# Loading a 512-element vector as four rows and transposing it with one matmul, in place of 512 loads of four bytes

## The chip, the cores and the metric

The kernel runs on one core of a Trainium2 chip. The metric is the device time of one execution in microseconds (us). Most repeated executions of one kernel scatter by a few tenths of a microsecond; some kernels here scatter by 2 to 4 us. "Faster" or "slower" needs 2%, which is 5.6 us here.

Engines are named as in the profile: PE is TensorE (matmuls; PEld is its weight loads), DVE is VectorE, ACT is ScalarE, POOL is GpSimd, SP is SyncE, which issues most DMA transfers. A "q" after the name (SPq, ACTq) means the engine's queue of instructions, where DMA issues stand.

## The reference, cut to what matters

```python
def _attn_ref(q, k, v):                    # 8 batches, 8 heads, 576 tokens, 64 wide
    q_s = softmax(q, axis=-1)              # written out in the reference
    k_s = softmax(k, axis=2)
    kv = np.einsum('bhsd,bhse->bhde', k_s, v)
    return np.einsum('bhsd,bhde->bhse', q_s, kv)

def _moe_ref(x, g_ln, w_ch1, w_ch2):       # x: 8 x 576 x 512
    mu, var = mean and variance of x over its last axis
    xn = (x - mu) / np.sqrt(var + 1e-06) * g_ln     # g_ln: 512 numbers
    ch = np.maximum(xn @ w_ch1, 0.0) @ w_ch2        # 512 -> 2048 -> 512
    return x + ch
```

## The kernel before

The kernel folds `g_ln` into the first weight matrix: row c of `w_ch1` is multiplied by 16 times g[c], and the mean over the rows is subtracted from the result, so that the tokens themselves need no centring. For that, g must lie down the partitions of SBUF, 128 numbers in each of four columns. The kernel fetches it that way, with four DMA transfers of 128 elements of four bytes:

```python
plan.add("POOL", 1.5, lambda: make_identity(nc, ident), w=["ident"])       # never read
...
for ko in range(KO1):                                                      # KO1 = 4, P = 128
    plan.add("ACT", 0.4, lambda ko=ko: nc.scalar.dma_start(
        g_sb[:, ko : ko + 1], moe_g_ln[ko * P : (ko + 1) * P, None]), w=[("g", ko)])
plan.add("POOL", 4.5, lambda: nc.gpsimd.tensor_scalar_mul(g_sb, in0=g_sb, scalar1=GS),
         r=[("g", ko) for ko in range(KO1)], w=[("g", ko) for ko in range(KO1)])
```

The kernel contains a planner. Every piece of work is added as a task with an engine, a believed duration, the keys it reads and writes, and a class `cls`. When all tasks are known, a greedy list scheduler walks through believed time and fixes the order of every engine; only then are the instructions emitted.

`fill` then puts matmuls of zeros ("fillers") into TensorE's believed idle times at the start; they are meant to keep its clock up.

Tasks:

```python
nc.tensor.matmul(pa[..], ek[..], vb[..])              # L379  key-value product ("kv"), into two banks pa
nc.vector.reciprocal(rz[..], pa[..])                  # L386  1/sum of exp(k)
nc.vector.tensor_scalar_mul(kve[..], pa[..], rz[..])  # L393  scaled kv
nc.vector.reduce_sum(zq[:, hf], eh, axis=AX.X)        # L331  row sums of exp(q), 1.35 us
nc.vector.tensor_tensor(w1, w1, nm, op=ALU.subtract)  # L292  subtracts the mean from a block of w1
nc.sync.dma_start_transpose(eqT[u], eq[u])            #       transposes exp(q) of batch 1, by DMA
nc.tensor.matmul(pa[..], kve[..], eqT[..])            # L405, L428 (last rows): transposed x of batch 1
nc.vector.tensor_copy(xsT[..], pa[..])                # L416  evacuates it
w2_sums: T[0..3] = differences of blocks of w2        # L566  three on VectorE, one on GpSimd
nc.tensor.matmul(pg[gis[j]], hT[..], w2_sb[..])       # L677  second layer of batch 0, 16 groups of 4 matmuls
nc.tensor.matmul(bank[gi], w1_sb[..], xt[..])         # L535  first layer
```

The kernel uses eight banks of PSUM, the memory that matmuls write: `pa[0..3]` and `pg[0..3]`. From batch 1 on, the second layer is done in another form (`mm2_split`, L615), in which VectorE evacuates (L625).

The softmax here doesn't subtract the row's maximum and nothing guards it: scores larger than these inputs give would overflow.

Of the kernel before, what the change touches and what calls it, by code (L numbers as in the profile page):

```python
# [12 lines left out]
FP32 = mybir.dt.float32  # L13
FP16 = mybir.dt.float16
# [125 lines left out]
def kernel(  # L140
# [10 lines left out]
    nc = tc.nc  # L151
# [3 lines left out]
    P = 128  # L155
# [5 lines left out]
    KO1 = DM // P  # L161
# [3 lines left out]
    GS = 16.0  # L165
# [4 lines left out]
    def sb(shape, dt, name):  # L170
        return persist.tile(shape, dt, name=name, tag=name)
# [1 line left out]
    w1_sb = sb([P, KO1, DH], FP16, "w1_sb")  # L173
    w2_sb = sb([P, KO2, DM], FP16, "w2_sb")
    g_sb = sb([P, KO1], FP32, "g_sb")
    ident = sb([P, P], FP16, "ident")
    zero = sb([P, 512], FP16, "zero")
    ones = sb([P, P], FP16, "ones")
    eps = sb([P, 1], FP32, "eps")
# [27 lines left out]
    pa = [psum.tile([P, 512], FP32, name=f"pa{i}", tag=f"pa{i}") for i in range(4)]  # L207

    plan = Plan()
# [9 lines left out]
    def init():  # L219
        plan.add("ACT", 1.3, lambda: nc.scalar.add_instruction(mybir.InstLoadActFuncSet(  # L220
            name=nc.get_next_instruction_name(), engine=mybir.EngineType.Activation, act_func_set_id=6)), cls=-1)
        plan.add("DVE", 0.3, lambda: nc.vector.memset(zero.bitcast(U32), 0), w=["zero"])  # L222
        plan.add("DVE", 0.1, lambda: nc.vector.memset(eps, 1e-6 * GS * GS), w=["eps"])
        plan.add("DVE", 0.1, lambda: nc.vector.memset(ones, 1.0 / DM), w=["ones"])
        plan.add("POOL", 1.5, lambda: make_identity(nc, ident), w=["ident"])
        for i in range(2):
            plan.add("POOL", 0.2, lambda i=i: nc.gpsimd.memset(vb[i][:, :, :, :, D], 1.0), w=[("vb", i, h, e) for h in range(2) for e in range(2)])
        for ko in range(KO1):
            plan.add("ACT", 0.4, lambda ko=ko: nc.scalar.dma_start(
                g_sb[:, ko : ko + 1], moe_g_ln[ko * P : (ko + 1) * P, None]), w=[("g", ko)])  # L230
        plan.add("POOL", 4.5, lambda: nc.gpsimd.tensor_scalar_mul(g_sb, in0=g_sb, scalar1=GS),
                 r=[("g", ko) for ko in range(KO1)], w=[("g", ko) for ko in range(KO1)])


    gate = [(), None]
# [465 lines left out]


    init()
    warmed = warm(12)
    state = {"eqT": (), "ev": []}
# [83 lines left out]
```

## Time and profile before

| | before |
|---|---|
| median of 3 runs (the fourth came with the result) | 281.96 us (281.94 to 282.53) |
| span of the profiled execution | 280.7 us |
| TensorE busy | 269.3 us (96%) |
| VectorE busy | 205.1 us (73%) |
| GpSimd busy | 12.6 us (5%) |

From the page of the kernel before, the 40 slices of the span (7.0 us each): busy tenths of TensorE and VectorE, and the rate of the DMA engines.

```profile
PE   8988898999999997999999999999999999999994
DVE  0988999899869874986598659966986683641573
GB/s 190 386 388 386 390 388 202 313 297 258 385 186 149 251 354 63 149 145 381 141 149 104 388 177 149 156 392 122 149 86 21 131 149 2 0 36 116 1 2 151
```

TensorE is full almost everywhere. From the second to the sixth slice the DMA engines bring weights and inputs at 386 to 390 GB/s, and VectorE is nearly full too; TensorE is busy as well, in part with fillers.

The timeline of the kernel before in its first microseconds (start, duration, engine, line, operation, tiles; in brackets the engine's idle time before the instruction and what ended it):

```profile
0.74 2.02 ACTq L229 DMA_DIRECT2D g_sb<-in_moe_g_ln_dram  x4
...
2.23 0.47 SPq L238 DMA_DIRECT2D stg<-in_q_dram  x1
5.77 0.89 SPq L238 DMA_DIRECT2D stg<-in_moe_w_ch_dram  x2
5.77 1.16 ACT L329 ACTIVATE eq<-stg 128x1152 bf16<-128x1152 f32 x1 [3.78 <-DMA stg<-in_q_dram]
...
9.34 1.39 POOL L231 TENSOR_SCALAR g_sb<-g_sb 128x4 f32<-128x4 f32 x1 [7.19 <-DMA g_sb<-in_moe_g_ln_dram]
```

The first q lands at about 5.75 us (ScalarE's exp starts at 5.77). GpSimd waits 7.19 us for g and is done at 10.73. The first block of w1 that needs g lands at 11.85 us, so GpSimd's multiply is on nobody's critical path.

VectorE's timeline a little later, in the kernel before:

```profile
11.41 0.16 DVE L386 RECIPROCAL rz<-pa 128x1 f32<-128x1 f32 x1
11.61 0.28 DVE L393 TENSOR_SCALAR kve<-pa,rz 128x64 f16<-128x64 f32 x1
...
12.34 0.16 DVE L386 RECIPROCAL rz<-pa 128x1 f32<-128x1 f32 x1
12.42 1.33 DVE L331 TENSOR_REDUCE zq<-eq 128x18 f32<-128x1152 bf16 x1
...
16.91 1.22 DVE L292 TENSOR_TENSOR w_sb<-w_sb,cp 128x2048 f16<-128x2048 f16 x1
```

The first mean is subtracted from w1 by 18.13 us.

TensorE's timeline in the stage, the second layer of batch 0, in the kernel before:

```profile
37.31 5.34 PE L677 MATMUL pg<-w_sb,hT 128*128 128x512 f16 x24
42.58 0.90 PE L379 MATMUL pa<-vb,ek 64*64 64x65 f16 x72
43.42 4.49 PE L677 MATMUL pg<-w_sb,hT 128*128 128x512 f16 x20
49.14 0.63 PE L405 MATMUL pa<-eqT,kve 64*64 64x512 bf16 x8 [1.23 <-DMA eqT<-eq]
...
51.37 0.25 PE L428 MATMUL pa<-eqT,kve 64*64 64x64 bf16 x6 [0.49 <-DVE xsT L416]
51.55 3.63 PE L677 MATMUL pg<-w_sb,hT 128*128 128x512 f16 x16
55.01 3.19 PE L535 MATMUL pa<-xsT,w_sb 128*128 128x512 f16 x14
```

The stage starts at 37.31 us. After 44 matmuls, which are 11 of the 16 groups, TensorE waits 1.23 us for the DMA transpose of exp(q), then 0.49 us for VectorE's evacuation (L416), and does the last 16 matmuls after that. At 55.01 us it can begin block 1, the first layer of batch 1.

### The profile page before, as it was taken

The page shows a single profiled execution, that of the slowest core. Times are in us where ns is not written, and L with a number is a line of the kernel's source. Part 1 is how long each engine was busy: PE and PEld are TensorE (multiplying, and loading weights), DVE is VectorE, ACT ScalarE, POOL GpSimd, SP SyncE. Part 2 cuts the span into 40 slices and gives each one's busy share as a digit, 9 for nine tenths or more (in the row PEclk, how much of TensorE's full clock was granted, in tenths as well). Part 3 has the DMA queues.
Part 4 walks back from the last instruction along what each step waited for, and adds up shares of the span by engine and source line. Part 5 has one row for each costly group of instructions (what it writes and reads, how often), then busy time and mean ns, then how long its engine had stood idle before and what let it go on. Part 6 is the DMA issues. An engine that isn't in the chain of part 4 may idle for free.

```text
span 280.7 us, 5656 instructions
## 1 busy us (share of the span) xinstructions
PE 269.3 (96%) x2317; PEld 163.8 (58%) x2317; DVE 205.1 (73%) x408; ACT 163.9 (58%) x267; POOL 12.6 (5%) x17
## 2 busy tenths in 40 slices
PE   8988898999999997999999999999999999999994
PEld 3443344445864486546854785478447844874583
DVE  0988999899869874986598659966986683641573
ACT  3567793298887594569655865695565067006500
POOL 2115007000000000000000000000000000000000
PEclk9999999999999999999999999999999999999998
DMA  6999999999958992569655995797543650013004
GB/s 190 386 388 386 390 388 202 313 297 258 385 186 149 251 354 63 149 145 381 141 149 104 388 177 149 156 392 122 149 86 21 131 149 2 0 36 116 1 2 151
DMA packets 58522, 55.36 MB, mean 197 GB/s; under 512 B 37248, under 2 KB 37760, under 8 KB 58496
## 3 DMA queue, kind: packets, MB, share of 16 engines
q1 hardware_dynamic: 57776, 54.86, 68.6%
q8 instruction: 18, 0.29, 0.4%
q10 hardware_dynamic: 720, 0.13, 0.3%
q14 instruction: 8, 0.07, 0.1%
HBM read 36.70 MB, written 9.44 MB: 164 GB/s over the span
## 4 chain that ended last, share of the span: by engine, by line
PE 73%; DMA 13%; DVE 9%; ACT 1%; POOL 1%; issue 1%; DVEq 0%
PE pg L535 37%; PE pg L615 28%; DMA stg<-in_moe_w_ch_dram 6%; DMA x<-xsT 5%; PE pg L677 3%; DVE T L566 2%; DMA stg<-in_q_dram 2%; DVE S L551 2%; DVE bst L487 1%; PE pa L379 1%; PE pa L615 1%; PE pa L535 1%; POOL w_sb L271 1%; DVE ot L625 1%; PE pa L405 1%
## 5 line engine op out<-in xcount | busy, mean ns | idle before, releaser
L498 ACT ACTIVATE hT<-pg 128x512 f16<-128x512 f32 x134 | 79.4, 596 | 73.4 <-PE pg L535 72.6
L535 PE MATMUL pg<-xsT,w_sb 128*128 128x512 f16 x488 | 108.1, 379 | 0.5 <-DVE w_sb L292 0.5
L535 PEld LDWEIGHTS <-w_sb 128*128 128x128 f16 x568 | 54.8, 98 | 65.6 <-DVE w_sb L292 1.5
L615 PEld LDWEIGHTS <-S 128*128 128x128 f16 x512 | 49.7, 98 | 5.9
L615 PEld LDWEIGHTS <-hT 128*128 128x128 f16 x384 | 37.0, 98 | 10.5 <-issue 5.0
L615 PE MATMUL pg<-T,S 128*128 128x256 f16 x368 | 42.5, 273 | 0.1
L551 DVE TENSOR_TENSOR S<-hT 128x1024 f16<-128x1024 f16 x32 | 22.0, 688 | 25.9 <-ACT hT L498 25.8
L625 DVE SCALAR_TENSOR_TENSOR cp<-pg,st,x 128x256 f32<-128x256 f32 x46 | 20.2, 479 | 13.7 <-PE pg L615 12.9
L615 PE MATMUL pg<-w_sb,hT 128*128 128x256 f16 x248 | 29.3, 273 | 0.0
L625 DVE SCALAR_TENSOR_TENSOR ot<-pg,st,cp 128x256 f32<-128x256 f32 x47 | 20.5, 478 | 9.9 <-PE pg L615 9.7
L487 DVE BATCH_NORM_STATS2 bst<-x 128x6 f32<-128x512 f16 x36 | 24.0, 668 | 4.9 <-DMA x<-xsT 4.8
L331 DVE TENSOR_REDUCE zq<-eq 128x18 f32<-128x1152 bf16 x16 | 21.5, 1344 | 5.7 <-ACT eq L329 5.7
L329 ACT ACTIVATE eq<-stg 128x1152 bf16<-128x1152 f32 x16 | 18.7, 1172 | 6.2 <-DMA stg<-in_q_dram 6.2
L335 DVE TENSOR_TENSOR eq<-eq,rzq 128x1152 bf16<-128x1152 bf16 x16 | 21.7, 1357 | 0.5
L356 ACT ACTIVATE ek<-stg 128x1152 bf16<-128x1152 f32 x16 | 18.6, 1169 | 1.5 <-DMA stg<-in_k_dram 1.5
L418 ACT CAST xsT<-pa 128x512 f16<-128x512 f32 x28 | 14.5, 595 | 4.7 <-PE pa L405 4.7
L368 ACT CAST vb<-stg 128x1152 f16<-128x1152 f32 x14 | 16.3, 1171 | 0.6 <-DMA stg<-in_v_dram 0.6
L615 PE MATMUL pg<-T,hT 128*128 128x256 f16 x120 | 14.4, 273 | 2.2 <-DVE ot L625 2.2
L615 PE MATMUL pg<-w_sb,S 128*128 128x256 f16 x128 | 15.3, 273 | 0.0
L696 PE MATMUL pg<-zero 128*128 128x512 f16 x47 | 13.4, 441 | 1.2 <-DVE zero L222 1.2
L677 PE MATMUL pg<-w_sb,hT 128*128 128x512 f16 x64 | 14.5, 380 | 0.0
L535 PE MATMUL pg<-xT,w_sb 128*128 128x512 f16 x64 | 14.0, 379 | 0.0
(67 smaller groups left out, 176.2 us busy)
## 6 DMA issues: line engine op xcount, KB each, us to landing
stg<-in_q_dram SPq DMA_DIRECT2D x16, 576.0 KB, 5.4
stg<-in_k_dram SPq DMA_DIRECT2D x16, 576.0 KB, 7.4
stg<-in_v_dram SPq DMA_DIRECT2D x16, 576.0 KB, 8.2
out_dram<-ot SPq DMA_DIRECT2D x33, 256.0 KB, 3.6
stg<-in_moe_w_ch_dram SPq DMA_DIRECT2D x16, 512.0 KB, 10.2
out_dram<-ot SPq DMA_DIRECT2D x1, 512.0 KB, 2.8
x<-xsT SPq DMA_TRANSPOSE x8, 6.7
out_dram<-ot SPq DMA_DIRECT2D x1, 128.0 KB, 2.7
```

Source lines behind the costliest of these rows:

```text
L329: plan.add("ACT", act_t(QW), lambda: nc.scalar.activation(e.rearrange("p j (s d) -> p s j d", s=2), sv(s), AF.Exp), r=sk(s), w=[("eq", u, ...
L331: plan.add("DVE", dve_t(QW), lambda: nc.vector.reduce_sum(zq[:, hf], eh, axis=AX.X), r=[("eq", u, hf)], w=[("zq", hf)], cls=qcls, after=sums_)
L335: plan.add("DVE", dve_t(QW), lambda: nc.vector.tensor_tensor(eh, eh, rzq[:, hf].to_broadcast([P, 2 * JT, D]), op=ALU.mult), r=[("rzq", hf) ...
L356: plan.add("ACT", act_t(QW), lambda: nc.scalar.activation(ek[u][:, hf].rearrange("p j (s d) -> p s j d", s=2), sv(s), AF.Exp), r=sk(s), w= ...
L368: plan.add("ACT", act_t(QW), lambda: nc.scalar.copy(vd, va), r=sk(s), w=[("vb", u, hf, i) for i in range(2)], cls=cls, slack=late, after=exps)
L487: plan.add("DVE", dve_t(512), lambda j=j: nc.vector.bn_stats(bst[:, j, :], x[:, j, :]), r=[(xk, j)], w=[("bst", j)], cls=cls, slack=2.0 if ...
L498: nc.scalar.activation(hT[:, m, :], bank, AF.Relu)
L535: nc.tensor.matmul(bank[gi], w1_sb[:, ko, m * P : m * P + P], xt[:, ko], start=(ko == 0), stop=(ko == KO1 - 1))
L551: plan.add("DVE", dve_t(256 * n, 2), lambda: nc.vector.tensor_tensor(S[i][:, ks], a, b, op=op), r=r, w=sk(i), cls=0.3 if k0 else 0.45)
L615: nc.tensor.matmul(g[i][0], fa(k, i), fb(k), start=(first and k == 0 and (i == 0 or g[0][1] != g[1][1])), stop=(last and k == HK - 1), ski ...
L625: nc.vector.scalar_tensor_tensor(dst[:, i, :], in0=g[i][0], scalar=sti[:, 4, 2 * t0 + i : 2 * t0 + i + 1], in1=src[:, i, :], op0=ALU.mult, ...
L677: nc.tensor.matmul(pg[gis[j]], hT[:, kk, j * P : j * P + P], w2_sb[:, kk, :], start=(kk == 0), stop=(kk == KO2 - 1))
```

## The change

The intent is to have g loaded as four rows of 512 contiguous bytes, to turn them with one small matmul, to let VectorE multiply by 16 straight from PSUM, and to drop an identity that nobody reads.

```diff
-    ident = sb([P, P], FP16, "ident")
+    g_row = sb([KO1, P], FP32, "g_row")
+    ident_g = sb([KO1, KO1], FP32, "ident_g")
...
-        plan.add("POOL", 1.5, lambda: make_identity(nc, ident), w=["ident"])
+        plan.add("POOL", 0.8, lambda: make_identity(nc, ident_g), w=["ident_g"])
...
-        for ko in range(KO1):
-            plan.add("ACT", 0.4, lambda ko=ko: nc.scalar.dma_start(
-                g_sb[:, ko : ko + 1], moe_g_ln[ko * P : (ko + 1) * P, None]), w=[("g", ko)])
-        plan.add("POOL", 4.5, lambda: nc.gpsimd.tensor_scalar_mul(g_sb, in0=g_sb, scalar1=GS),
-                 r=[("g", ko) for ko in range(KO1)], w=[("g", ko) for ko in range(KO1)])
+        plan.add("ACT", 0.4, lambda: nc.scalar.dma_start(g_row, moe_g_ln.rearrange("(ko ki) -> ko ki", ki=P)), w=["g_row"], land=2.5)
+        plan.add("PE", 0.1, lambda: nc.tensor.transpose(pa[3][:, :KO1], g_row, ident_g), r=["g_row", "ident_g"], w=[("pa", 3)])
+        plan.add("DVE", 0.2, lambda: nc.vector.tensor_scalar_mul(g_sb, in0=pa[3][:, :KO1], scalar1=GS),
+                 r=[("pa", 3)], w=[("g", ko) for ko in range(KO1)])
```

## The prediction

> **What bounds the kernel before.** (1) From 5 to 42 us the loads: the 40 slices show 386 to 390 GB/s, and loads of w1 and w2 land one every 1.36 us (11.85, 13.22, ... 45.53 us). (2) VectorE is nearly full from 7 to 52 us. (3) From 30.4 us TensorE works almost without a gap; the timeline shows idle times of 1.23 us (at 49.14, waiting for the DMA transpose of eq), 0.49 (51.37), 0.41 (81.38) and 1.84 (111.65, an evacuation that stands on VectorE behind statistics waiting for a DMA transpose). A gain at the start counts only where it moves the ends of those gaps.
>
> **Removed.** Four issues on ScalarE's queue (0.49 us each), 512 packets of 4 bytes (9 ns each), a GpSimd multiply (1.39 us, ending at 10.73) and an unused identity. GpSimd's wait for g (7.2 us) cost nothing: g_sb is ready at 10.73 us, and the first w1 lands at 11.85.
>
> **Added.** One load of 4 rows, one tiny matmul, one VectorE multiply of 128x4 (0.2 us). In the order of instructions they stand behind 26 filler matmuls and the cast of vb, so g_sb is ready at about 10.7 us again: no gain from g itself.
>
> **DMA start.** Between 2.5 and 4.75 us the trace has packets of q and of g one for one (18/18, 19/19, 12/12, 14/14 per quarter microsecond), which fits the Trainium skill, "DMA: Bandwidth & Descriptors", section on queues, rings and completion order: an engine takes turns between queue rows packet by packet. The loads need 3 us from their first packet to full rate; after later pauses 1.25 to 1.75. If g's packets do that, all loads come about 0.8 us earlier (estimate); if it is only a cold start, 0. I take 0.5.
>
> **Moved.** The kernel's planner believed GpSimd busy for 4.5 us; without that it reorders everything up to 115 us. Propagating the trace's durations through the new order:
> - First block of w1: subtracting its mean now stands on VectorE behind the scaling of block 1 (landing at 20.1), so first-layer matmuls start later (about 2 us at 32 us).
> - That is absorbed, for TensorE waits at 49.1 us anyway for the transpose of eq, which the DMA queue ends 3.56 us after the last w2 load (45.53).
> - But only 9 instead of 11 of the 16 groups of the first second-layer product (0.87 us each) now stand before that wait. The 1.23 us gap grows to 2 us or more and 1.74 us of work comes after it; the 0.49 us gap goes. Token block 1 starts at 56.1 instead of 55.0 us, less the DMA gain.
> - At 81 us a product fills the 0.41 us gap; an earlier transpose of x takes 0.2 us off the 1.84.
>
> Sum: +1.1 (to 1.6) - 0.5 - 0.4 - 0.2, about +0.2.
>
> **Prediction:** 282.2 us, 80% within 280.8 to 283.6. Chances: faster 0.03, same 0.94, slower 0.03.
>
> **What would show it.** First q load landing at about 5 us instead of 5.75, all landings earlier by the same; g_sb written near 10.7; the first subtraction of the mean ending near 21 instead of 18.1; TensorE's gap at 49 us over 2 us; none at 81; the gap at 112 slightly smaller; steady stages unchanged (28 us per block).
>
> **What would make it wrong.** A DMA start unmoved (+0.5) or moved by over 1 us; the transpose of eq issued after 44.5 us, so that the delay isn't absorbed (+1 to 2); x transposes that close the 1.84 us gap (-1.5).

## More of the kernel before

```python
# Plan.order(), cut
t0 = max(free[eng], min(ready[i] for i in lst))                  # engine's next start
c = min((i for i in lst if ready[i] <= t0 + 1e-9), key=...)      # best class among the READY tasks
```

So a task of the best class that is ready 0.1 us too late loses its turn to whatever is ready.

SyncE issues four loads by 2.70 us and its fifth only at 5.77.

## The result, and the profile after

| | before | after |
|---|---|---|
| median, runs of the same rounds | 282.12 us (281.94 to 282.53, 4 runs) | 283.50 us (283.32 to 284.15, 4 runs) |
| ratio of fast runs, 95% interval | | 1.0051 (1.0031 to 1.0071): "same" |
| span of the profiled execution | 280.7 us | 281.5 us |

Ratios are the mean time of one kernel's fast runs over the mean of the other's fast runs of the same rounds, so they are not quite the ratio of the medians. The range of the prediction held, by 0.1 us. But the change was to be about neutral, and it costs 1.4 us. The interval excludes 1, so there is something to explain.

The first microseconds after:

```profile
0.74 0.55 ACTq L229 DMA_DIRECT2D g_row<-in_moe_g_ln_dram  x1
...
2.85 1.14 SPq L238 DMA_DIRECT2D stg<-in_moe_w_ch_dram  x2
...
4.67 1.16 ACT L329 ACTIVATE eq<-stg 128x1152 bf16<-128x1152 f32 x1 [2.68 <-DMA stg<-in_q_dram]
...
9.34 0.22 PE L230 MATMUL pa<-ident_g,g_row 4*128 4x4 f32 x1
...
9.60 0.16 DVE L231 TENSOR_SCALAR g_sb<-pa 128x4 f32<-128x4 f32 x1
```

The load does what it should: q lands 1.1 us earlier, SyncE issues on without a stop (the fifth load at 2.85 instead of 5.77 us; these two turn out to have different causes, see before_1dma), and g is ready at 9.76 us instead of 10.73.

VectorE after:

```profile
11.19 1.34 DVE L331 TENSOR_REDUCE zq<-eq 128x18 f32<-128x1152 bf16 x1
...
13.26 0.16 DVE L386 RECIPROCAL rz<-pa 128x1 f32<-128x1 f32 x1
13.46 0.28 DVE L393 TENSOR_SCALAR kve<-pa,rz 128x64 f16<-128x64 f32 x1
...
20.15 1.22 DVE L292 TENSOR_TENSOR w_sb<-w_sb,cp 128x2048 f16<-128x2048 f16 x1
```

Here the row sums stand before the reciprocals. They start 1.2 us earlier than before, but the reciprocal is 1.85 us later, and the mean of w1's first block is subtracted by 21.37 us instead of 18.13. This is another order of work, not a slower instruction.

TensorE in the second layer of batch 0, after:

```profile
38.37 2.75 PE L677 MATMUL pg<-w_sb,hT 128*128 128x512 f16 x12
...
43.71 3.63 PE L677 MATMUL pg<-w_sb,hT 128*128 128x512 f16 x16
49.00 0.63 PE L405 MATMUL pa<-eqT,kve 64*64 64x512 bf16 x8 [1.67 <-DMA eqT<-eq]
...
51.03 0.25 PE L428 MATMUL pa<-eqT,kve 64*64 64x64 bf16 x6 [0.28 <-DVE xsT L416]
51.21 5.35 PE L677 MATMUL pg<-w_sb,hT 128*128 128x512 f16 x24
56.40 1.89 PE L535 MATMUL pa<-xsT,w_sb 128*128 128x512 f16 x8
```

The stage starts 1.06 us later, the transposed exp(q) arrives at the same time as before (49.00 against 49.14), only 36 matmuls instead of 44 stand before that wait, and 24 instead of 16 after L428. Block 1 starts at 56.40 us, 1.39 us later. The sum is exact: eight matmuls more after L428 are 5.19 - 3.46 = 1.73 us from the start of that row of matmuls to block 1, and L428 was released 0.34 us earlier.

The rest of the kernel gives a part back. The wait of 0.41 us at 81 us is gone, that at 112 us is 1.56 instead of 1.84 us, and from the start of block 3 to the last matmul both kernels take the same (163.72 and 163.73 us). The starts of the stages in the traces that are compared below:

| trace | stage starts | L405 | L428 released | block 1 | block 3 | last matmul ends |
|---|---|---|---|---|---|---|
| before | 37.31 | 49.14 | 51.37 | 55.01 | 113.39 | 277.12 |
| before_again | 37.23 | 49.49 | 51.29 | 54.94 | 112.82 | 276.65 |
| after | 38.37 | 49.00 | 51.03 | 56.40 | 113.84 | 277.56 |
| bank | 36.57 | 48.43 | 50.64 | 54.28 | 112.03 | 275.84 |
| late_kv | 38.91 | 49.48 | 51.57 | 56.94 | 114.20 | 277.93 |
| before_late2 | 38.43 | 49.05 | 51.69 | 55.33 | 113.49 | 277.21 |

### The profile page after: what moved, and what is told of

The parts are those of the page before. It is cut to its first block, busy times and chain, and to the rows that moved or that the text cites. A ratio compares the mean times of both kernels' runs of the same rounds, so it can differ in the third digit from the quotient of the medians.

```text
span 281.5 us, 5669 instructions
## 1 busy us (share of the span) xinstructions
PE 270.8 (96%) x2327; PEld 164.7 (58%) x2327; DVE 204.9 (73%) x409; ACT 163.9 (58%) x267; POOL 11.0 (4%) x16
## 4 chain that ended last, share of the span: by engine, by line
PE 83%; DMA 12%; DVE 3%; ACT 1%; issue 0%; SPq 0%; DVEq 0%
PE pg L535 41%; PE pg L615 31%; DMA stg<-in_moe_w_ch_dram 4%; PE pg L677 3%; DMA x<-xsT 3%; DMA eqT<-eq 2%; PE pa L379 2%; DMA stg<-in_k_dram 2%; PE pa L405 2%; PE pa L615 1%; PE pa L535 1%; DVE w_sb L292 1%; PE pg L513 1%; DVE w_sb L274 1%; DVE cp L284 0%; PE pa L428 0%
## 5 line engine op out<-in xcount | busy, mean ns | idle before, releaser
L696 PE MATMUL pg<-zero 128*128 128x512 f16 x56 | 15.6, 433 | 1.2 <-DVE zero L223 1.2
L677 PE MATMUL pg<-w_sb,hT 128*128 128x512 f16 x64 | 14.7, 380 | 0.0
```

The source lines that it names most:

```text
L677: nc.tensor.matmul(pg[gis[j]], hT[:, kk, j * P : j * P + P], w2_sb[:, kk, :], start=(kk == 0), stop=(kk == KO2 - 1))
```

## The experiments

### First the planner: why is there another order at all?

The prediction said that the order changed because the planner no longer believes GpSimd busy for 4.5 us. This can be tried without a chip, by building. With that belief changed to anything from 0.2 to 3.5 us, the kernel before keeps its order on all engines. The step is wrong.

The cause is the PSUM bank. The change borrows `pa[3]` for the transpose of g, and the first kv product needs `pa[2]` and `pa[3]`. In the planner's own times kv then starts at 10.53 instead of 10.33 us and its reciprocal is ready at 11.17 instead of 10.97. The row sums are ready at 11.08. Before, the reciprocal was ready first and went first; now it is 0.09 us late, the scheduler gives VectorE to the row sums for 1.35 us, and much of what follows falls into another place. The traces of before and late_kv differ in their order up to about 85 us, not up to 115 as the prediction had it. Two builds show it. They also separate the two effects of the change, so both were run.

**bank** is the new load with the transpose in `pg[0]`, which nobody needs then. Its order on every engine is that of before, except for g's own instructions and one filler.

```diff
-  nc.tensor.transpose(pa[3][:, :KO1], g_row, ident_g)  ... w=[("pa", 3)]
+  nc.tensor.transpose(pg[0][:, :KO1], g_row, ident_g)  ... w=[("pg", 0)]
```

**late_kv** is the old load with the first kv product believed ready 0.2 us later. Its order is that of after.

```diff
-  slack=SLACK if steady else 0.2
+  slack=SLACK if steady else 0.4 if kind == "first" and hs == [0] else 0.2
```

They ran together with each kernel unchanged.

> The new load of g with the transpose put into bank pg[0] instead of pa[3]; by the built programs every engine then has the order of the kernel before (g's own instructions and fillers aside). Theory (the loss comes from the new order, which hangs on the borrowed bank, and the new load itself is a small gain): 281.5 to 282.1 us, that is 0.0 to 0.6 us below before and about 1.5 us below the changed kernel; first q load lands at 4.65 us as in the changed kernel; matmuls of the first layer run on without a break from about 30.0 us. Rival 1 (the new load, the float32 matmul or its place among the fillers costs by itself): 283 us or more, as the changed kernel. Rival 2 (all is noise between builds): within 0.3 us of both, no sign.

> The kernel before, loads of four bytes and all, with one number of its planner changed (it believes the first kv matmul 0.2 us later), which by the built programs gives every engine the order of the changed kernel. Theory (order alone loses): 283.3 to 284.2 us, 1.3 to 2.0 us above before, slightly above the changed kernel; first q load at 5.75 us; break of TensorE at 49 us 1.3 us or more, unbroken first-layer matmuls from about 31.8 us. Rival 1 (the load costs): 282.1 us as before. Rival 2 (noise): within 0.3 us of before.

> The kernel before, unchanged, for a second trace and for what two builds of one program differ by: ratio 1.000 within 0.002. Theory and rivals agree, except that rival 2 (noise) would have it differ by 1 us or more.

> The changed kernel, unchanged, in five rounds beside the others: 283.5 us, 1.2 to 1.6 us above before. First q load again at 4.65 us; the loads' lead over before again shrinks from 1.1 us at the first to about 0.4 us by 12 us (if the shrinking was chance, it stays near 1 us).

| kernel | load, order | median (range) | ratio to before, 95% |
|---|---|---|---|
| before (11 runs) | old, old | 282.10 (281.68 to 282.45) | |
| bank | new, old | 281.79 (281.53 to 281.99) | 0.9989 (0.9977 to 1.0001) |
| late_kv | old, new | 283.32 (282.95 to 283.50) | 1.0041 (1.0028 to 1.0054) |
| before_again | old, old | 281.96 (281.89 to 282.47) | 0.9999 (0.9987 to 1.0011) |
| after_again | new, new | 284.49 (282.70 to 285.90) | 1.0085 (1.0050 to 1.0119) |

The order alone costs 1.2 us in the medians (late_kv against before) and the load alone gains 0.3 us. bank differs from the changed kernel in nothing but the bank, and late_kv from before in nothing but the order. So the loss is an accident of scheduling, which the change triggered by borrowing a bank; the new load is innocent. Its own gain of 0.3 us is not clear of noise in the totals, for the interval of bank reaches 1.0001.

TensorE in late_kv, which has the old load, in the second layer of batch 0:

```profile
38.91 2.75 PE L677 MATMUL pg<-w_sb,hT 128*128 128x512 f16 x12
...
49.48 0.63 PE L405 MATMUL pa<-eqT,kve 64*64 64x512 bf16 x8 [1.59 <-DMA eqT<-eq]
...
51.57 0.25 PE L428 MATMUL pa<-eqT,kve 64*64 64x64 bf16 x6 [0.35 <-DVE xsT L416]
51.75 5.35 PE L677 MATMUL pg<-w_sb,hT 128*128 128x512 f16 x24
```

Again 24 matmuls stand after L428, as in after.

after_again spread over 3.2 us, which was not expected. Three of its six runs had a mean granted clock of 0.993 or 0.994, and these took 285.34 to 285.90 us; the others, at 0.997 to 1.0, took 282.70 to 283.65. (A mean of 0.997 need not matter: the trace of before has it too, and its half-rate stretch starts at 279.12 us, after the last matmul.) The trace of after_again is one of the three. Two stretches of it around 21 us (busy time of TensorE and its count of matmuls, then the granted clock, the DMA share and the rate):

```profile
18.00:21.30 3.30, 1.55 (x41) 1.00 1.05 388
21.30:24.71 3.41, 3.29 (x8) 0.50 1.05 387
```

For 3.41 us TensorE ran at half clock, after it had been idle from 18.31 to 19.63 us and again before 21.42. The Trainium skill, "TensorE: Matmul & The Clock Gate", section "What's actually happening", describes this: a free-running window of about 3.4 us, and half rate after an idle one. The window's length and the half rate agree with the trace. That the stretch before must be idle does not: TensorE was busy for 1.55 of its 3.30 us. Some runs are hit and some are not, as the six show, and other kernels are hit too (one run of before at a clock of 0.994 took 283.20 us). The four runs of the first measurement of after had clocks of 0.999 to 1.0, so its 283.50 us contain hardly any of this, and the 1.4 us must be explained without it.

### Is it the number of groups before the wait?

The prediction put the loss down to 9 instead of 11 groups before the wait at 49 us. In the planner, the believed landing time of that transpose decides how many groups are put ahead. Believed 2.6 instead of 0.6 us, after has 11 groups there, and bank has 14.

```diff
-  land=3.5 if steady else 0.6
+  land=3.5 if steady else 2.6        # transpose of exp(q), batch 1
```

> The changed kernel with one number of its planner changed (it believes that the first transpose of eq lands 2 us later), so that again 11, not 9, of the 16 groups of the first second-layer product stand before TensorE's wait for that transpose; the order up to there stays the changed kernel's. Theory (the loss is what the order puts behind that wait): the break at 49 us falls from 1.67 us to under 0.4, the first matmul of token block 1 starts at about 55 us instead of 56.4, time 281.9 to 282.6 us where no clock drop falls in, that is near the kernel before. Rival (the later start of the first layer, 31.45 against 30.39 us, is the loss): the time stays at 283.3 us or more.

> The kernel of run bank with the same planner number changed, which puts 14 of the 16 groups before the wait. Theory: the break of 1.26 us at 48.4 us goes, at most 0.5 us comes back because fewer matmuls cover the evacuations after it; 280.3 to 281.2 us, 0.6 to 1.5 below bank. Rival (a later wait sets the pace, as the statistics at 111 us): 281.5 us or more, with the break there larger by what was gained.

Both missed. after_l26 took 285.40 us (284.55 to 288.71), 1.0139 (1.0102 to 1.0176) of before; bank_l26 took 281.55 us (280.90 to 281.77), 0.9980 (0.9967 to 0.9993). In both the wait for the DMA is gone. But in after_l26 a longer wait for VectorE stands right behind it. TensorE in after_l26:

```profile
49.05 0.63 PE L405 MATMUL pa<-eqT,kve 64*64 64x512 bf16 x8
...
52.83 0.25 PE L428 MATMUL pa<-eqT,kve 64*64 64x64 bf16 x6 [2.03 <-DVE xsT L416]
53.01 5.31 PE L677 MATMUL pg<-w_sb,hT 128*128 128x512 f16 x16
```

and VectorE in after_l26, just before the evacuation that L428 waits for:

```profile
50.42 0.88 DVE L566 TENSOR_TENSOR T<-w_sb,T 128x512 f16<-128x512 f16 x2
51.22 0.42 DVE L566 TENSOR_TENSOR T<-w_sb 128x512 f16<-128x512 f16 x1
51.74 0.43 DVE L566 TENSOR_TENSOR T<-w_sb,T 128x512 f16<-128x512 f16 x1
52.09 1.28 DVE L416 CAST xsT<-pa 128x512 f16<-128x512 f32 x2
```

L405 was done with its eight matmuls by 49.7 us. The evacuation stood behind differences of w2 which nobody needs before the next stage: the planner, believing the transpose late, had put them ahead. The 16 matmuls after it take 5.31 us instead of 3.63 (before), because in this trace the clock is at half from 53.30 to 56.71 us, again after a stretch that was not idle (1.38 us busy in the 3.41 us before). At full rate block 1 would start at about 56.5 us (an estimate: 53.01 plus the 3.46 us of before), as in after. So this run moved the loss and did not remove it; its two runs at a clock of 1.0 still took 284.55 and 284.83 us, and what costs them the rest is open. In bank_l26 the same number moved the waits to 57.8 us (1.19 us, VectorE's output work) and 75.4 us (0.89 us). A belief changed by hand doesn't only move the one task it belongs to. Block 1 of bank_l26 did start at 53.03 instead of 54.28 us, as expected; the gain was returned within 22 us, in waits for VectorE.

**after_fill** put eight fillers into the idle times of after at 18 to 21 us.

```diff
+  if kind == "first" and hs == [1]: zeros(pg[3], True)(6)    # ahead of the second kv product
+  if m == 0: zeros(pg[3], True)(2)                           # ahead of the first layer's first matmuls
```

> The changed kernel with eight more filler matmuls, six ahead of the second kv product and two ahead of the first-layer matmuls, where TensorE stood idle for 1.05 to 1.31 and 0.55 us. Theory of the spread (the runs at 285 to 286 us are those in which the granted clock falls to a half for one window of 3.4 us after that idle stretch): no run with a mean clock under 0.996, all runs within 283.0 to 283.9 us. Rival (the spread comes from the DMA or elsewhere): again some runs above 285 us.

It missed too: it took 283.80 us (283.51 to 285.40). The idle times at 19.6 and 21.4 us are gone from its trace, but one of six runs still had a clock of 0.994 and took 285.40, and two at 0.999 and 1.0 took 284.64 and 284.09, so the clock is not all of the spread. One run of six at a low clock against three of six is too little to call the half-rate windows rarer, and they are not the explanation of the 1.4 us.

### Is it the number of transfers or the number of elements that holds the start up?

**before_1dma** fetches the same 512 elements of four bytes with one transfer.

```diff
-  for ko in range(KO1): nc.scalar.dma_start(g_sb[:, ko : ko + 1], moe_g_ln[ko * P : (ko + 1) * P, None])
+  nc.scalar.dma_start(g_sb, moe_g_ln.rearrange("(ko ki) -> ki ko", ki=P))
```

> The kernel before with the 512 elements of four bytes loaded by one DMA instead of four; every engine keeps its order. Theory (the packets of four bytes slow the start of the loads): q lands again at about 5.7 us, time 282.0 us as before. Rival (the four issues, or the waits of the queues that four more DMAs in flight bring, slow it): q lands at 4.4 to 4.7 us, as with the four rows. A q between them would say that both do.

It took 282.11 us (281.95 to 282.57), 1.0008 (0.9995 to 1.0020). The first q lands at 5.61 us, as in the old load (5.49 to 5.77 in four traces) and not as in the new (4.42 to 4.99 in seven). Yet SyncE's fifth load is issued at 2.79 us, as in the new load: the stop of SyncE goes with the four transfers, the late q with the small elements. The rates say the same. In before the DMA engines move 138 GB/s from 2.50 to 4.25 us, in after 366; in before_1dma, where the small elements come a little later, the rate falls to 56 from 4.00 to 4.50 us. So the many small elements delay the first loads, not the issuing. This agrees with what the prediction quoted from the Trainium skill, "DMA: Bandwidth & Descriptors", section on queues, rings and completion order: engines take turns between queues packet by packet. In before the trace shows such turns (18 packets on each of the two queues from 2.75 to 3.00 us); in before_1dma, from 4.00 to 4.25 us, they are 9 to 76, so the turns need not be one for one.

### Does the wait absorb a late start of the stage?

After these runs a rival theory looked strong. In four traces of the old order, block 1 started 17.70 or 17.71 us after the start of the stage; in four of the new, 18.03 us. If this distance was rigid, because VectorE's work in this stage hangs on the stage's own kv product, then the later start would pass through in full, and the prediction's word "absorbed" would be the failed step. **before_late** tests this: five matmuls of zeros, 1.1 us, ahead of the stage, in the kernel before.

```diff
   for kk in range(k0, k0 + 4):        # preceded, for c == 0, k0 == 0, j == 0, by
+      zeros(pg[gis[0]], True)(5)
```

> The kernel before with five zero matmuls (about 1.1 us of TensorE) put directly ahead of the first group of the first second-layer product, and nothing else; this imitates the later start of that product in the changed kernel without the other load and without the other order. Theory A (the chain of VectorE work that begins with the key-value product inside this stage sets when block 1 may start, and it moves with the start of the stage): the stage starts at about 38.4 instead of 37.3 us, the distance from there to block 1 stays 17.70 us, and the kernel takes about 1.1 us longer at block 3 as well as at the end of the chain of TensorE, about 283.0 to 283.3 us in all. Theory B, that of the prediction (the wait at 49 us is for a DMA that lands at its own time, so it absorbs a late start): the wait shrinks from 1.2 to 1.7 us to under 0.6 us, the distance is about 16.6 us, and the time is within 0.2 us of before.

The four timed runs took 282.37 us in the median (282.15 to 282.68), 1.0011 (0.9999 to 1.0024). The profiled execution took 1583 us, with every 128x512 matmul at about 1.7 us throughout, instead of one every 0.216 us. The clock is listed as 1.0, but this trace holds no record of a granted clock at all (its page has no PEclk line). It shows no stage and is left out; what happened in it is open. So the kernel ran once more.

> The same kernel as before_late, once more, for a trace: the profiled execution of before_late ran every matmul some eight times too slow, so that it shows no stage, while its four timed runs took only about 0.3 us more than before, where 1.1 us of work was added. What is to be told apart is where the other 0.8 us went. Theory A1: the late start passes the wait at 49 us in full (17.70 us from the start of the stage to block 1, which starts at about 56.0 us) and is taken up later, in the waits at 81 and 111 us (block 3 then starts at 113.1 us or earlier, as against 112.8 to 113.4 us in the two traces of before). Theory B: the wait at 49 us takes it up (distance about 16.6 us, block 1 starts at about 55.0 us). Time again 282.2 to 282.6 us under both.

It took 282.39 us (282.32 to 282.61), 1.0007 (0.9993 to 1.0021). TensorE in before_late2 (what is L677 in the other kernels is L679 here, two inserted lines later):

```profile
38.43 5.34 PE L679 MATMUL pg<-w_sb,hT 128*128 128x512 f16 x24
...
49.05 0.63 PE L405 MATMUL pa<-eqT,kve 64*64 64x512 bf16 x8
...
51.69 0.25 PE L428 MATMUL pa<-eqT,kve 64*64 64x64 bf16 x6 [0.90 <-DVE xsT L416]
51.87 3.63 PE L679 MATMUL pg<-w_sb,hT 128*128 128x512 f16 x16
55.33 2.97 PE L535 MATMUL pa<-xsT,w_sb 128*128 128x512 f16 x13
```

The stage starts at 38.43 us, as late as in after. The wait of 1.23 us before L405 has shrunk to 0.09 us, VectorE takes up the rest by being late itself, and block 1 starts at 55.33 us, only 0.32 us later than before: 16.90 us after the stage's start. The rival theory falls, and the prediction's "absorbed" holds for 0.8 of 1.1 us. The constant distance had misled: it was constant because nothing in those traces moved one end alone.

This run also gives the cleanest comparison. before_late2 and after start the stage together (38.43 and 38.37) and get the transposed exp(q) together (49.05 and 49.00). after is released at L428 0.66 us earlier, and yet starts block 1 1.07 us later. The two groups that the new order left for later, 1.73 us, make the whole difference.

### VectorE and GpSimd in the same stage

VectorE's differences of w2 (L566) take 0.42 us, but some take 1.37. The group of this line in bank (number of instructions; shortest, median and longest in ns; first and last start):

```profile
L566 DVE TENSOR_TENSOR T<-w_sb,T x8: 411/446/1369, 43.4 to 51.1; 128x512 f16<-128x512 f16 x8
L566 POOL TENSOR_TENSOR T<-w_sb x4: 1156/1297/1337, 42.4 to 47.0; 128x512 f16<-128x512 f16 x4
```

**bank_t3** and **bank_t3_l26** let VectorE compute GpSimd's four differences too, in bank and in bank_l26.

```diff
-  eng, e = ("POOL", nc.gpsimd) if i == 2 else ("DVE", nc.vector)
+  eng, e = "DVE", nc.vector
```

> bank with the four differences of w2 that GpSimd computes given to VectorE. Theory A (two engines compete for SBUF there: three differences on VectorE take 1.37 us instead of 0.42 us while GpSimd runs its own): every difference on VectorE takes 0.41 to 0.45 us, VectorE's chain between the key-value product and the evacuations of the transposed x gets about 1.6 us shorter (2.85 less, 1.26 more), the 0.47 us wait before the ninth rows' product at 50.6 us goes, and block 1 starts about 0.45 us earlier, 17.25 us after the start of the stage. In the total 0.3 to 0.5 us, 281.3 to 281.5 us. Rival: the long ones are long for another reason (their operands), stay at 1.37 us, and block 1 starts over 1 us later because VectorE has more to do.

> bank_l26 (14 groups of the first second-layer product ahead of the wait) with the four differences of w2 that GpSimd computes given to VectorE. In bank_l26 the gain was given back, 1.19 us at 57.8 us and 0.89 us at 75.4 us, where TensorE waited for VectorE. If VectorE is late there because of the competition with GpSimd, the first of these falls below 0.4 us and the kernel takes 280.2 to 281.0 us, about 0.5 to 1.0 us less than bank_l26. If not, it stays at 281.5 us.

The same group in bank_t3:

```profile
L566 DVE TENSOR_TENSOR T<-w_sb x8: 415/417/419, 33.3 to 54.8; 128x512 f16<-128x512 f16 x8
L566 DVE TENSOR_TENSOR T<-w_sb,T x8: 393/416/419, 43.6 to 55.2; 128x512 f16<-128x512 f16 x8
```

With GpSimd quiet, none is long. That part is shown, and it agrees with the Trainium skill, "SBUF — State Buffer", section "Who interferes with whom": a VectorE instruction with two inputs in SBUF contends with a GpSimd instruction that reads SBUF. The wait before L428 disappeared and block 1 started 17.27 us after the stage's start (17.25 had been expected). The total did not follow: 282.38 us (281.32 to 283.54), 1.0012 (0.9988 to 1.0036). Two of its six runs had a clock of 0.993 or 0.994 and took 283.54 and 283.30; the other four took 281.32 to 282.74, about as bank does. A new wait of 2.49 us for VectorE stands at 76.5 us in its trace. The build shows that the planner had moved other work too; that this makes the wait is argued, not shown. bank_t3_l26 had a median of 281.53 us over all six runs; one run at a clock of 0.95 is put aside as slow, and the five fast ones took 280.40 to 281.75 us, 0.9969 (0.9953 to 0.9985). Its profile is that slow run, so its waits are not compared and its expectation, which was about a wait, stays undecided. It is as good as bank_l26 within the intervals. These two are the only kernels whose interval lies below 1 against before, by 0.2 and 0.3%.

### The end of the kernel

One term was found by reading the traces only. From the start of the last store's issue, which is on ScalarE's queue, to the end of the span, the traces with four transfers of g on that queue take 3.05 to 3.07 us (four traces), and those with one transfer 3.25 to 3.54 us (eight traces in the fast state; after and bank 3.4). The data of that store go out equally fast, the last packet 1.8 us after the issue starts, in before, late_kv, before_1dma, after, bank and bank_l26; what follows is the program's own closing instructions on all engines. before_1dma has the old elements and one transfer, and takes 3.4 us: so it goes with the number of transfers, not with the size of the elements. Why the closing takes longer is open.

## Why the prediction was right or wrong

Its range held; its centre of 282.2 us was 1.3 us low. That 283.50 lies under the upper end of 283.6 is in part luck: the second measurement of the same kernel, after_again, came to 284.49 us. The parts, one by one:

- **"What would show it", first item: q at about 5 us.** Right in direction; it came earlier still, at 4.65 instead of 5.75 us. "All landings earlier by the same" was wrong. The first w1 lands at 11.47 instead of 11.85 us, the last w2 at 45.05 instead of 45.53. A lead of 1.1 us becomes one of 0.4 to 0.5. The traces show where it goes: from 9 to 10 us the loads run at 226 to 251 GB/s in all seven fast traces of the new load, and at 386 to 407 in the five fast traces with the old elements. Why the rate falls there is open. The prediction had named a move of q by over 1 us as something that would make it wrong; q did move by 1.10, and the 0.5 us came out all the same, since a later loss that it had not seen took the rest: block 1 starts 0.66 us earlier in bank than in before_again, and 0.54 earlier in after than in late_kv.
- **"g_sb is ready at about 10.7 us again."** It was ready at 9.76 us. As predicted, this was worth nothing, since w1 lands later.
- **"The planner believed GpSimd busy for 4.5 us; without that it reorders everything."** Wrong cause. The borrowed PSUM bank delayed a task by 0.2 us in the plan and cost it its turn. That the order changes, and how, had been read correctly from the build: the first subtraction of a mean ended at 21.37 us ("near 21").
- **"That is absorbed."** Right for 0.8 of 1.1 us (before_late2). The rival theory about it was what fell.
- **"Only 9 instead of 11 groups": +1.1 us at block 1.** The mechanism was right and the term was too small. (The gap before L405 was to be over 2 us; it is 1.67 in after and 1.59 in late_kv.) late_kv, which has the new order without the new load, starts block 1 at 56.94 us instead of the predicted 56.1. The prediction let the wait before L428 go; it stayed (0.35 us in late_kv, 0.28 in after), since VectorE is full there and has L416 behind the differences of w2. It also took the landing of exp(q)'s transpose from one trace, 49.14 us, where late_kv and before_again have 49.48 and 49.49. In late_kv that is not scatter: the transpose lands 3.92 us after the last w2 load, not the 3.56 that the prediction carried over from before. This distance is 3.56 or 3.57 us in the seven fast traces that begin with the old order, and 3.91 to 3.96 in four of the five that begin with the new (4.26 in after_again, whose clock dropped); why is open. The wait before L428 and the later landing make 0.7 of the 0.84 us; the rest is not accounted for.
- **"At 81 us ... 0.4, an earlier transpose takes 0.2": given back later.** About right. Between block 1 and block 3 the new order gains 0.62 us (late_kv against before_again, 57.26 and 57.88 us).
- **Not in the prediction:** 0.35 us more at the end of the kernel.

In the traces, up to the issue of the last store, the order costs 1.28 us (late_kv against before_again, 278.48 and 277.20 us), and the load gains 0.36 us (after at 278.12 against late_kv). The longer end costs 0.35 us. That sums to 1.27 us, and the medians show 1.38. These are single pairs of traces, and two traces of the same kernel differ by 0.47 us at this point (before at 277.67 us, before_again at 277.20), so only the signs are safe. In this pair nearly all of the load's gain was spent on the last 3 us of the kernel, where nobody had looked; in bank against before_again (276.40 and 277.20 us) the gain is 0.80 us and under half of it was.

## What to carry to other kernels

When an order is made by a greedy planner, a temporary buffer is a scheduling decision: borrow a bank that nobody needs at that time, and compare the order of instructions on each engine before the time. A wait that "absorbs" a delay should be tested by moving one end alone, with a few dummy matmuls; a distance that is constant over many traces proves nothing while nothing has pulled at it. And a small gain at the start has to be followed to the last instruction, for it can be lost anywhere on the way, even after the last store has been issued.

## What the Trainium skill lacked or had wrong

- "DMA: Bandwidth & Descriptors": it says that engines take turns between queues by packet, but no figure of what many tiny elements do to other loads at a kernel's start. Here 512 elements of four bytes held back the first load of q by 1.1 us (5.75 against 4.65 us), in four transfers as in one (5.61 us). 40 us later, at the last w2 load, 0.5 us of that was left (45.53 against 45.05 us); with one transfer of the same elements it landed at 45.19 us, so how much of this remainder is due to the elements and how much to the number of transfers is not shown.
- No page has the time from the issue of a program's last store to the end of its span, or says what changes it. Here it was 3.05 to 3.07 us with four transfers on ScalarE's queue at the start, and 3.25 to 3.54 us with one.
- "SBUF — State Buffer" has the contention of VectorE and GpSimd right: 0.42 us became 1.37 us for a 128x512 difference while GpSimd computed one.
- "TensorE: Matmul & The Clock Gate" has the length and the half rate of the window right: 3.41 us at a granted clock of 0.50. But it puts the half rate after an idle window, and here it came after stretches in which TensorE was busy for 1.55 of 3.30 us and for 1.38 of 3.41 us. Its caveats on a stuck clock do not reach as far as one execution of 1583 us, in which matmuls of 128x512 took 1.7 us each and no granted clock was recorded.
